# Fifteen one-element reads on GpSimd and a new program order in a fused attention and MLP kernel

## The chip, the cores and the metric

The kernel runs on one core of a Trainium2 chip. The core has five engines, each with its own instruction stream: TensorE (PE) for matrix products, VectorE (DVE) and ScalarE (ACT) for elementwise work, GpSimd (POOL) and SyncE (SP), which here mostly issue DMA transfers. An engine works through its own list in order and waits on semaphores for others. The metric is the time of one execution on the device in microseconds (us), as the median of several runs; one more execution is profiled, and its trace is what the rows below come from.

## The reference

```python
def _attn_ref(q, k, v, n_sink, window):          # q, k, v: (4, 8, 768, 64) f32
    scores = scale * np.matmul(q, k.transpose(0, 1, 3, 2))
    is_sink = pos[None, :] < int(n_sink)         # n_sink = 4
    rel = pos[:, None] - pos[None, :]
    in_window = (rel >= 0) & (rel < int(window)) # window = 128
    scores = np.where(is_sink | in_window, scores, -1e9)
    ...                                          # softmax over the last axis: a
    return np.matmul(a, v)

x = attn_out.transpose(0, 2, 1, 3).reshape(3072, 512)
h = x @ w_in                                     # (512, 2048)
P = a[0] + a[1] * h + a[2] * h**2 + a[3] * h**3
Q = 1.0 + abs(b[0]) * abs(h) + abs(b[1]) * h**2
out = (P / (Q + 1e-6)) @ w_out                   # (2048, 512)
```

Attention with a window of 128 positions and four sink positions, then a layer whose nonlinearity is a quotient of two polynomials, over 4 x 768 = 3,072 tokens.

## The kernel before

The work is cut into 12 steps `s` of 256 tokens, three to a batch. For each step the attention part runs ahead of the matrix part by a step or more:

- `load_q`, `load_k`, `load_v` (L333, L364, L371, and L346, L355, L380 for the first steps) are DMA transfers issued by GpSimd, which cast f32 to bf16 on the way, as do `load_w_in` (four quarters, L412) and `load_w_out` (four, L418). q and k are turned by PE in the first steps (L536) and later by DMA transposes that SyncE issues (`turn_q` L587, `turn_k` L591).
- `scores(s, 0..3)` on PE (L622, L632) puts products of k and q into PSUM and adds the mask by further matmuls (L640); `exps(s, 0..3)` on ACT (L652) takes them to bf16; `attend(s, 0..1)` on PE (L693) multiplies by v; `norm(s, 0..1)` on DVE (L701, L702) divides by the sum and writes the tile `x_n`; `turn_x` (L722, L727 on PE, L740 by DMA from step 5 on) makes `xblk`, the left side of the matrix part.
- `gemm1(m, 0..3)` on PE (L752) is x @ w_in in four quarters of 16 matmuls, each evicted by `copy_in(m, j)` on ACT (L759) into the tile `hb`. The nonlinearity is a chain on DVE and ACT: `sqa`/`sqd` (h squared, ACT L766 or DVE L768), `and` (|h|, L773), `den` (L777), `even` (L782), `odd` (L786), `odd_h` (L790), `num` (L793) on DVE, `ln` (L796) and `exp` (L801) on ACT for the reciprocal, `gate` (L806) on DVE. `gemm2(m, ...)` on PE (L813) is the product with w_out, `copy_out` (L825) its eviction, `store` the transfer to `out`.

`x_n`, `hb`, `sq`, `den`, `g` and `xblk` have two buffers each, `num` has one; a step's tile is written over the tile of two steps before. PSUM is four pools of two banks, `ps_h`, `ps_o`, `ps_m` and `ps_s`; table `BANK` says which pool a product takes.

No scheduler sets the order. Each piece of work is declared with `piece(name, engine, ...)`, which gives it a number; the table `ORDER` is a list of these numbers, and the program is written piece by piece in that order (a negative number -n is n empty matmuls, `spin`). The order of pieces of one engine in `ORDER` is that engine's order of work. Table `ENGINE` says whether a copy goes to DVE or ACT. Semaphores follow from the tiles that a piece reads and writes.

Of the kernel before, what the change touches and what calls it, by code (L numbers as in the profile page):

```python
# [61 lines left out]
def kernel(  # L62
# [42 lines left out]
    V_PE = 3  # L105
    KB = 3
# [7 lines left out]
    ENGINE = {('cast_k0', 0): 'ACT',  # L114
               ('cast_q0', 0): 'DVE',
               ('cast_q0', 1): 'DVE',
               ('place_k0', 0): 'ACT',
               ('place_k0', 1): 'DVE',
               ('place_kc', 2, None): 'ACT',
               ('place_kc', 3, None): 'ACT',  # L120
               ('place_qc', 2, None): 'ACT',
               ('place_qc', 3, 0): 'ACT',
               ('place_vc', 1): 'DVE',
# [3 lines left out]
               ('placed_x', 1, 0): 'DVE',  # L127
               ('placed_x', 2, 0): 'DVE',
               ('placed_x', 4, 0): 'DVE',
               ('placed_x', 4, 1): 'DVE'}  # L130
    BANK = {('attend', 0, 1): 'ps_o',
             ('attend', 2, 0): 'ps_o',
             ('attend', 2, 1): 'ps_h',
             ('attend', 3, 0): 'ps_o',
             ('attend', 3, 1): 'ps_h',
             ('attend', 4, 0): 'ps_o',
# [3 lines left out]
             ('attend', 8, 0): 'ps_o',  # L140
# [5 lines left out]
             ('gemm1', 0, 2): 'ps_o',  # L146
             ('gemm1', 0, 3): 'ps_m',
             ('gemm1', 1, 0): 'ps_m',
             ('gemm1', 1, 1): 'ps_m',
             ('gemm1', 2, 1): 'ps_h',  # L150
# [5 lines left out]
             ('gemm1', 4, 0): 'ps_m',  # L156
# [4 lines left out]
             ('gemm1', 5, 3): 'ps_m',  # L161
             ('gemm1', 6, 0): 'ps_o',
# [6 lines left out]
             ('gemm1', 8, 2): 'ps_o',  # L169
             ('gemm1', 9, 1): 'ps_m',  # L170
# [6 lines left out]
             ('gemm1', 11, 0): 'ps_o',  # L177
# [4 lines left out]
             ('gemm2', 11, 0, 0): 'ps_o',  # L182
             ('scores', 0, 2): 'ps_h',
             ('scores', 1, 1): 'ps_m',
             ('scores', 1, 2): 'ps_o',
             ('scores', 2, 2): 'ps_m',
             ('scores', 2, 3): 'ps_o',
             ('scores', 3, 0): 'ps_h',
             ('scores', 3, 2): 'ps_h',
             ('scores', 4, 1): 'ps_m',  # L190
             ('scores', 4, 3): 'ps_h',
             ('scores', 5, 2): 'ps_o',
             ('scores', 6, 0): 'ps_o',
             ('scores', 6, 2): 'ps_h',
             ('scores', 7, 1): 'ps_o',
             ('scores', 8, 0): 'ps_m',
             ('scores', 8, 1): 'ps_h',
             ('scores', 9, 2): 'ps_h',
# [3 lines left out]
             ('scores', 11, 0): 'ps_m',  # L202
             ('turn_k0', 0): 'ps_h',
             ('turn_k0', 1): 'ps_o',
             ('turn_kc', 2, None): 'ps_h',
             ('turn_kc', 3, None): 'ps_h',
             ('turn_q0', 0): 'ps_m',
             ('turn_qc', 1, None): 'ps_o',
             ('turn_qc', 2, None): 'ps_h',
             ('turn_qc', 3, 0): 'ps_h',  # L210
             ('turn_vc', 1): 'ps_h',
             ('turn_vc', 2): 'ps_h',
             ('turn_vs', 1): 'ps_h',
             ('turn_x', 0, 0): 'ps_o',
             ('turn_x', 0, 1): 'ps_o',
# [3 lines left out]
             ('turn_x', 2, 1): 'ps_h',  # L219
             ('turn_x', 4, 0): 'ps_o',  # L220
# [35 lines left out]
    nil = const_pool.tile([P, 1], FP32, name="nil")  # L256
    sel = const_pool.tile([P, 2, NTS, 64], BF16, name="sel")
# [147 lines left out]
    def place_vc(s, eng):  # L405
        b, g = divmod(s, GPB)
        copy(eng, v_fix[b % 2][:, g * NHF:(g + 1) * NHF, :, 0:D],
             ps_v2.pop(s).rearrange("p j (h d) -> p j h d", d=D))

# [614 lines left out]
    for s in range(NSTEP):  # L1024
# [44 lines left out]
        for G in range(2):  # L1069
# [14 lines left out]
                   ("turned_x", s - 2) if s >= 2 else None], frees=home)  # L1084
        gs = range(2)
        piece(("attended", s), "NONE", 0.0, 0, None, [("attend", s, G) for G in gs])
# [28 lines left out]
    def every(nm, m):  # L1115
        return [(nm, m, p_) for p_ in range(parts(m))] if m >= 0 else []

    for m in range(NSTEP):
        r_ = 4 * m
        old = m - 2  # L1120
        for j in range(4):
            home = bank_of(("gemm1", m, j), ("ps_h", "ps_o")[j % 2])
            piece(("gemm1", m, j), "PE", 1.76, r_ + j,
                  lambda m=m, j=j, home=home: project_in(m, j, home),
                  [("turned_x", m), ("load_w_in", j)], takes=home)
            piece(("copy_in", m, j), "ACT", on_act(GW), r_ + j + 0.25,
                  lambda m=m, j=j: copy_in(m, j),
                  [("gemm1", m, j)] + every("odd_h", old)
                  + ([("turn_vc", s_) for s_ in range(V_PE)] + [("turn_kc", 3, None)]
                     if m == 1 else []),  # L1130
                  frees=home)
# [114 lines left out]
```

## Time and profile before

| | us |
|---|---|
| median of 3 runs | 247.15 (245.81 to 248.28) |
| profiled execution | 248.32 |
| its span, first to last instruction | 246.6 |
| busy in it: PE / DVE / ACT / POOL | 221.3 / 217.1 / 209.7 / 81.5 |

The profiled execution's own time is 1.7 us longer than its span. PE's busy time is that of pipelined matmuls whose ends are modelled, so a busy PE is not PE at its peak. In rows of a timeline the first number is the start, the second the time covered, `xN` the number of equal instructions merged, and the bracket at the end the idle time before the row and what ended it; `issue` means that the profile shows nothing that was waited for.

### The profile page before, as it was taken

What the parts mean: (1) busy time and instruction counts of PE and PEld (TensorE: products, weight loads), DVE (VectorE), ACT (ScalarE), POOL (GpSimd) and SP (SyncE); (2) the same over time, 40 slices, a digit from 0 to 9 for tenths busy, and PEclk for the clock granted to TensorE, in tenths of its full rate; (3) what the DMA queues carried; (4) which work ended last, traced back from release to release, by engine and by line L of the source; (5) the groups of instructions that cost most, each with busy time, mean ns of one, the idle gap of its engine ahead of it and who ended that gap; (6) DMA issues with size and microseconds to landing.
All of it is one profiled execution on the core that took longest, in us unless ns stands there. A gap on an engine that the chain in (4) does not pass through costs nothing.

```text
span 246.6 us, 7309 instructions
## 1 busy us (share of the span) xinstructions
PE 221.3 (90%) x3253; PEld 147.0 (60%) x3253; DVE 217.1 (88%) x252; ACT 209.7 (85%) x173; POOL 81.5 (33%) x111
## 2 busy tenths in 40 slices
PE   1787887995999999699999989999999999999992
PEld 0465665793766667457658647757657668554430
DVE  4977784898779999987898999999999999999991
ACT  2186795998599998978989996999999999999950
POOL 8619567556463896060079600000000000000000
PEclk9999997999799999999999999999999999999999
DMA  7999999999999999999299993053301024000422
GB/s 190 158 184 140 190 181 112 108 101 175 203 156 124 151 186 116 108 173 63 40 96 239 146 98 66 3 66 122 94 3 21 3 44 171 1 3 0 170 85 85
DMA packets 95375, 26.98 MB, mean 109 GB/s; under 512 B 86128, under 2 KB 92272, under 8 KB 95344
## 3 DMA queue, kind: packets, MB, share of 16 engines
q0 software_dynamic: 65024, 12.98, 83.5%
q1 hardware_dynamic: 28792, 12.61, 31.1%
q10 hardware_dynamic: 1528, 0.93, 1.5%
q8 instruction: 25, 0.41, 0.7%
q14 instruction: 6, 0.05, 0.1%
HBM read 27.30 MB, written 6.29 MB: 136 GB/s over the span
## 4 chain that ended last, share of the span: by engine, by line
DVE 44%; PE 34%; issue 8%; ACT 7%; DMA 3%; POOL 1%; SPq 1%; DVEq 0%; POOLq 0%
PE ps_m L752 8%; PE ps_h L813 8%; DVE sq L790 7%; DVE num L793 7%; DVE den L777 5%; PE ps_o L752 5%; DVE g L806 5%; DVE num L782 3%; DMA qT<-q_bf 3%; DVE sq L786 3%; DVE x_n L702 3%; DVE sq L768 3%; ACT hb L759 3%; DVE den L773 2%; PE ps_h L752 2%
## 5 line engine op out<-in xcount | busy, mean ns | idle before, releaser
L752 PEld LDWEIGHTS <-w_in_sb 128*128 128x128 bf16 x768 | 74.5, 99 | 18.3 <-issue 6.2
L813 PE MATMUL ps_h<-w_out_sb,g 128*128 128x512 bf16 x288 | 66.2, 379 | 0.0
L813 PEld LDWEIGHTS <-g 128*128 128x128 bf16 x384 | 36.4, 98 | 42.1 <-DVE g L806 2.6
L796 ACT ACTIVATE lnq<-den,one_eps,qsc 128x4096 f32<-128x4096 bf16 (+1 forms) x18 | 48.3, 2682 | 0.0
L801 ACT ACTIVATE den<-lnq 128x4096 bf16<-128x4096 f32 (+1 forms) x18 | 45.0, 2502 | 0.1
L752 PE MATMUL ps_m<-xblk,w_in_sb 128*128 128x256 bf16 x352 | 43.7, 279 | 0.0
L371 POOL DMA_DIRECT2D v<-in_v_dram x48 | 35.1, 748 | 13.2 <-DVE v L283 7.8
L752 PE MATMUL ps_o<-xblk,w_in_sb 128*128 128x256 bf16 x320 | 38.3, 273 | 0.4 <-ACT hb L759 0.4
L806 DVE TENSOR_TENSOR g<-num,den 128x4096 bf16<-128x4096 bf16 (+1 forms) x18 | 28.3, 1571 | 1.4 <-ACT den L801 1.3
L777 DVE TENSOR_TENSOR den<-den,sq 128x4096 bf16<-128x4096 bf16 (+1 forms) x18 | 28.3, 1573 | 0.8 <-ACT sq L766 0.5
L790 DVE TENSOR_TENSOR sq<-sq,hb 128x4096 bf16<-128x4096 bf16 (+1 forms) x18 | 28.2, 1573 | 0.2
L793 DVE TENSOR_TENSOR num<-num,sq 128x4096 bf16<-128x4096 bf16 (+1 forms) x18 | 28.3, 1572 | 0.1
L759 ACT ACTIVATE hb<-ps_m 128x1024 bf16<-128x1024 f32 x22 | 22.8, 1037 | 6.1 <-PE ps_m L752 6.1
L333 POOL DMA_DIRECT2D q_bf<-in_q_dram x15 | 15.7, 1049 | 32.5 <-DMA qT<-q_bf 27.9
L652 ACT ACTIVATE e<-ps_s 128x768 bf16<-128x768 f32 (+1 forms) x26 | 23.3, 895 | 1.5 <-PE ps_s L640 1.5
L759 ACT ACTIVATE hb<-ps_o 128x1024 bf16<-128x1024 f32 x20 | 20.9, 1047 | 2.0 <-PE ps_o L752 1.9
L766 ACT ACTIVATE sq<-hb 128x1024 bf16<-128x1024 bf16 (+1 forms) x15 | 20.4, 1363 | 0.1
L768 DVE TENSOR_TENSOR sq<-hb 128x2048 bf16<-128x2048 bf16 (+2 forms) x13 | 16.9, 1302 | 2.9 <-ACT hb L759 2.9
L786 DVE TENSOR_SCALAR sq<-sq,acoef 128x4096 bf16<-128x4096 bf16 (+1 forms) x18 | 18.0, 1005 | 0.3
L782 DVE TENSOR_SCALAR num<-sq,acoef 128x4096 bf16<-128x4096 bf16 (+1 forms) x18 | 18.0, 1003 | 0.0
L364 POOL DMA_DIRECT2D k_bf<-in_k_dram x16 | 14.2, 898 | 9.6 <-DMA w_out_sb<-in_moe_w_out_dram 3.5
L773 DVE TENSOR_SCALAR den<-hb 128x2048 uint32<-128x2048 uint32 (+1 forms) x18 | 15.9, 881 | 0.4 <-ACT hb L759 0.4
(131 smaller groups left out, 261.9 us busy)
## 6 DMA issues: line engine op xcount, KB each, us to landing
out_dram<-o_t SPq DMA_DIRECT2D x11, 512.0 KB, 4.8
w_in_sb<-in_moe_w_in_dram POOLq DMA_DIRECT2D x4, 512.0 KB, 9.9
k_bf<-in_k_dram POOLq DMA_DIRECT2D x16, 128.0 KB, 8.0
w_out_sb<-in_moe_w_out_dram POOLq DMA_DIRECT2D x4, 512.0 KB, 14.4
q_bf<-in_q_dram POOLq DMA_DIRECT2D x15, 128.0 KB, 7.8
v<-in_v_dram POOLq DMA_DIRECT2D x24, 64.0 KB, 7.5
stage_v<-in_v_dram POOLq DMA_DIRECT2D x3, 256.0 KB, 8.0
v<-in_v_dram POOLq DMA_DIRECT2D x24, 32.0 KB, 6.6
```

Source lines behind the costliest of these rows:

```text
L371: nc.gpsimd.dma_start(out=v_fix[b % 2][half(r), g * NHF:(g + steps) * NHF, hl, 0:D], in_=v[b, h, g * TS:(g + steps) * TS, :].rearrange("(j ...
L752: nc.tensor.matmul(ps[:, n, :], lhsT=w_in_all[:, c, fc * P:(fc + 1) * P], rhs=xblk[m][:, c, :], start=(c == 0), stop=(c == NDMC - 1))
L759: nc.scalar.activation(out=hb[m][:, j * GW:(j + 1) * GW], in_=ps_h.pop((m, j)).rearrange("p n c -> p (n c)"), func=AF.Copy)
L777: nc.vector.tensor_tensor(out=den[m][:, c], in0=den[m][:, c], in1=sq[m][:, c], op=ALU.add)
L782: nc.vector.tensor_scalar(out=num[m][:, c], in0=sq[m][:, c], scalar1=a2, scalar2=a0, op0=ALU.mult, op1=ALU.add)
L786: nc.vector.tensor_scalar(out=sq[m][:, c], in0=sq[m][:, c], scalar1=a3, scalar2=a1, op0=ALU.mult, op1=ALU.add)
L790: nc.vector.tensor_tensor(out=sq[m][:, c], in0=sq[m][:, c], in1=hb[m][:, c], op=ALU.mult)
L793: nc.vector.tensor_tensor(out=num[m][:, c], in0=num[m][:, c], in1=sq[m][:, c], op=ALU.add)
L796: nc.scalar.activation(out=lnq_fix[:, c], in_=den[m][:, c], func=AF.Ln, scale=qsc, bias=one_eps)
L801: nc.scalar.activation(out=den[m][:, c], in_=lnq_fix[:, c], func=AF.Exp, scale=-1.0)
L806: nc.vector.tensor_tensor(out=g_of[m][:, c], in0=num[m][:, c], in1=den[m][:, c], op=ALU.mult)
L813: nc.tensor.matmul(ps_out[m][:, tt, :], lhsT=g_of[m][:, co:co + P], rhs=w_out_all[:, fc, :], start=(fc == 0), stop=(fc == NFFC - 1))
```

## The change

GpSimd gets 15 new instructions: `hold("x", s)` for steps 0 to 7 copies one element of `x_n` of step s into a small tile `seen`, and `hold("h", m)` for steps 0 to 6 one element of `hb`. Each stands somewhere between GpSimd's load issues. So GpSimd goes no further before `norm(s, 0)` and `norm(s, 1)`, or the four `copy_in(m, j)`, have written their tile; and `norm(s + 2)` and `copy_in(m + 2)`, which write over it, come after the hold. The table `ORDER` is another one throughout (its numbers also shift, since the holds are numbered among the pieces), and tables `ENGINE` and `BANK` change in some rows. There are 3 empty matmuls (`spin`) in place of 19.

```diff
@@ ORDER @@
-    3, 109, 127, 113, 118, -6, 1, 0, 125, 2, 108, 128, 126, 107, 14, 4, 15, 116, 119, 117, 146, 5,
...
+    3, 108, 126, 1, 2, 125, 128, 109, 117, 127, 113, 118, 0, 14, 15, 107, 146, 5, 110, 4, 16, 119,
...
+    HOLD_X = tuple(range(8))
+    HOLD_H = tuple(range(7))
...
-    ENGINE = {('cast_k0', 0): 'ACT',
-               ('cast_q0', 0): 'DVE',
+    ENGINE = {('cast_q0', 0): 'DVE',
                ('cast_q0', 1): 'DVE',
-               ('place_k0', 0): 'ACT',
-               ('place_k0', 1): 'DVE',
+               ('place_k0', 1): 'ACT',
                ('place_kc', 2, None): 'ACT',
                ('place_kc', 3, None): 'ACT',
+               ('place_qc', 0, 0): 'ACT',
+               ('place_qc', 0, 1): 'ACT',
...
-               ('place_vc', 1): 'DVE',
                ('place_vc', 2): 'DVE',
...
+               ('placed_x', 1, 1): 'DVE',
                ('placed_x', 2, 0): 'DVE',
+               ('placed_x', 2, 1): 'DVE',
+               ('placed_x', 3, 1): 'DVE',
...
+    seen = const_pool.tile([1, 2 * NSTEP], BF16, name="seen")
...
+    def hold(kind, s):
+        t_ = x_n[s][0:1, 1, 0:1] if kind == "x" else hb[s][0:1, MW - 1:MW]
+        at = 2 * s + (kind == "x")
+        nc.gpsimd.tensor_copy(out=seen[:, at:at + 1], in_=t_)
...
             piece(("norm", s, G), "DVE", 0.97, 4 * s + at - 5 - 0.1,
                   lambda s=s, G=G: normalize(s, G),
                   [("attend", s, G), ("scale_x",),
-                   ("turned_x", s - 2) if s >= 2 else None], frees=home)
+                   ("turned_x", s - 2) if s >= 2 else None,
+                   ("hold", "x", s - 2) if s - 2 in HOLD_X else None], frees=home)
...
+        if s in HOLD_X:
+            piece(("hold", "x", s), "POOL", 0.2, 4 * s, lambda s=s: hold("x", s),
+                  [("norm", s, 0), ("norm", s, 1)])
...
                   [("gemm1", m, j)] + every("odd_h", old)
+                  + ([("hold", "h", old)] if old in HOLD_H else [])
...
+        if m in HOLD_H:
+            piece(("hold", "h", m), "POOL", 0.2, r_ + 4, lambda m=m: hold("h", m),
+                  [("copy_in", m, j) for j in range(4)])
```

Three places show what the new order moves. The line numbers of the changed kernel are higher by 10 to 15 there.

The first is PE where the first of the long stops fell: 1,214 instructions into its list, in the last mask matmuls of `scores(3, 2)`. Before, `gemm1(0, 3)` follows there; with the change `gemm1(0, 3)` stands ahead of `scores(3, 2)`, and its end falls on that count. ACT's list shows the same exchange in the rows that empty the two products: `copy_in` has `hb<-`, `exps(3, ...)` has `e_1_96` or `e_1_94`. Before:

```order
L766 ACTIVATE sq<-hb 128x1024
L652 ACTIVATE e_1_96<-ps_h 128x2x384
L759 ACTIVATE hb<-ps_m 128x1024
L652 ACTIVATE e_1_94<-ps_s 128x2x384
L652 ACTIVATE e_1_94<-ps_h 128x2x512
L801 ACTIVATE den<-lnq 128x1024
L759 ACTIVATE hb<-ps_m 128x1024
L796 ACTIVATE lnq<-den,one_eps,qsc 128x1024
```

With the change:

```order
L811 ACTIVATE lnq<-den,one_eps,qsc 128x1024
L816 ACTIVATE den<-lnq 128x1024
L774 ACTIVATE hb<-ps_h 128x1024
L667 ACTIVATE e_1_96<-ps_s 128x2x384
L774 ACTIVATE hb<-ps_o 128x1024
L811 ACTIVATE lnq<-den,one_eps,qsc 128x1024
L667 ACTIVATE e_1_94<-ps_s 128x2x384
L667 ACTIVATE e_1_94<-ps_h 128x2x512
```

`copy_in(0, 3)` now comes ahead of `exps(3, 2)`, and `copy_in(1, 0)` ahead of the other two `exps`, as `gemm1(1, 0)` does on PE; they stood behind them.

The second is GpSimd with the loads of v for steps 3 and 4. `v_1` is the v tile of the odd batches; the 64x4x64 loads into it are those of step 3 (one for each head), the 64x8x64 ones of step 4. Before:

```order
L371 DMA v_1_92<-in_v_dram 64x4x64
L333 DMA q_bf_1212<-in_q_dram 128x8x64
L371 DMA v_1_92<-in_v_dram 64x4x64
L371 DMA v_1_92<-in_v_dram 64x8x64 x7
L418 DMA w_out_sb_106<-in_moe_w_out_dram 128x4x512 x4
L364 DMA k_bf_1456<-in_k_dram 128x8x64
```

With the change, from `hold("x", 2)` to the last three quarters of w_out:

```order
L423 COPY seen_117<-x_n_1079 1x1
L381 DMA v_1_92<-in_v_dram 64x8x64
L381 DMA v_1_92<-in_v_dram 64x4x64 x2
L381 DMA v_1_92<-in_v_dram 64x8x64
L381 DMA v_1_92<-in_v_dram 64x4x64 x2
L433 DMA w_out_sb_106<-in_moe_w_out_dram 128x4x512
L423 COPY seen_117<-hb_697 1x1
L381 DMA v_1_92<-in_v_dram 64x8x64 x4
L423 COPY seen_117<-hb_1052 1x1
L423 COPY seen_117<-x_n_1428 1x1
L381 DMA v_1_92<-in_v_dram 64x8x64
L433 DMA w_out_sb_106<-in_moe_w_out_dram 128x4x512 x3
```

Four loads of v step 3 stand behind `hold("x", 2)`, and three quarters of w_out behind `hold("h", 0)`, `hold("h", 1)` and `hold("x", 3)` as well.

The third is ACT around `ln(3)` (`lnq<-den`) and `exp(3)` (`den<-lnq`). The `hb` rows are `copy_in`, the `e_1_94` rows `exps(7, ...)`, the `o_t` row `copy_out(2)`. Before, the first row is `copy_in(4, 3)`, the third `copy_in(4, 2)`:

```order
L759 ACTIVATE hb<-ps_o 128x1024
L796 ACTIVATE lnq<-den,one_eps,qsc 128x4096
L759 ACTIVATE hb<-ps_m 128x1024
L652 ACTIVATE e_0_95<-ps_s 128x2x384
L801 ACTIVATE den<-lnq 128x4096
L652 ACTIVATE e_1_94<-ps_o 128x2x384
L652 ACTIVATE e_1_94<-ps_s 128x2x512
L825 ACTIVATE o_t<-ps_h 128x1024
```

With the change the first two rows are `copy_in(4, 3)` and `copy_in(4, 2)`, the fifth `copy_in(5, 3)`:

```order
L774 ACTIVATE hb<-ps_o 128x1024
L774 ACTIVATE hb<-ps_m 128x1024
L811 ACTIVATE lnq<-den,one_eps,qsc 128x4096
L816 ACTIVATE den<-lnq 128x4096
L774 ACTIVATE hb<-ps_o 128x1024
L840 ACTIVATE o_t<-ps_h 128x1024
L667 ACTIVATE e_1_94<-ps_m 128x2x512
L667 ACTIVATE e_1_94<-ps_s 128x2x384
```

`copy_in(4, 2)`, `exp(3)` and a quarter of step 5 stand ahead of the first `exps(7, ...)`; on PE `gemm1(4, 2)`, `gemm1(5, 3)` and the first half of `gemm2(2, 1)` stand likewise ahead of `scores(7, 1)`, which stood ahead of `gemm1(4, 2)`.

## Rows read from the trace of the kernel before

**Rows 1.** The page's first lines: the span, then busy us of each engine.

```profile
span 246.6 us, 7309 instructions
PE 221.3 (90%) x3253; PEld 147.0 (60%) x3253; DVE 217.1 (88%) x252; ACT 209.7 (85%) x173; POOL 81.5 (33%) x111
```

**Rows 2.** Windows: stretch, length, busy PE, PEld, DVE, ACT, POOL, clock, DMA, GB/s.

```profile
24.00:70.00 46.00, 39.28 (x816) 30.22 (x814) 34.99 (x59) 36.32 (x42) 27.09 (x34) 0.93 1.95 153
70.00:150.00 80.00, 76.78 (x1146) 49.98 (x1144) 75.37 (x64) 75.02 (x54) 39.33 (x48) 1.00 1.87 128
150.00:240.00 90.00, 89.26 (x959) 56.10 (x957) 88.56 (x79) 86.36 (x63) 0.00 (x0) 1.00 0.20 57
```

**Rows 3.** The timeline of DVE: four rows of norm from 20 to 70 us.

```profile
20.91 0.75 DVE L702 SCALAR_TENSOR_TENSOR x_n<-ps_m,ratio,rec 128x512 bf16<-128x512 f32 x1
...
42.98 0.21 DVE L701 RECIPROCAL rec<-ps_o 128x8 f32<-128x8 f32 x1 [3.05 <-PE ps_o L693]
...
48.13 0.75 DVE L702 SCALAR_TENSOR_TENSOR x_n<-ps_h,ratio,rec 128x512 bf16<-128x512 f32 x1
...
69.45 0.21 DVE L701 RECIPROCAL rec<-ps_o 128x8 f32<-128x8 f32 x1 [3.34 <-PE ps_o L693]
```

**Rows 4.** The timeline of PE: two gemm1 pieces and the four stops.

```profile
28.94 1.92 PE L752 MATMUL ps_o<-xblk,w_in_sb 128*128 128x256 bf16 x16
...
38.52 0.35 PE L640 MATMUL ps_h<-nege,ident 64*64 64x256 bf16 x2 [1.54 <-issue]
38.80 3.49 PE L752 MATMUL ps_m<-xblk,w_in_sb 128*128 128x256 bf16 x16
...
46.36 0.27 PE L632 MATMUL ps_s<-qT,kT 64*64 64x192 bf16 x2 [0.41 <-issue]
...
61.63 2.53 PE L752 MATMUL ps_h<-xblk,w_in_sb 128*128 128x256 bf16 x15 [2.51 <-issue]
...
147.34 0.25 PE L693 MATMUL ps_o<-v,e 64*64 64x65 bf16 x6 [1.03 <-issue]
```

**Rows 5.** Windows up to the first two stops, and behind the first.

```profile
0.00:38.50 38.50, 25.37 (x607) 18.86 (x607) 29.35 (x74) 23.95 (x30) 24.43 (x43) 1.00 1.45 173
0.00:46.30 46.30, 32.80 (x735) 23.92 (x735) 33.99 (x83) 28.73 (x36) 28.61 (x48) 0.96 1.59 160
...
39.90:43.00 3.10, 3.10 (x80) 2.19 (x78) 0.05 (x2) 0.67 (x1) 2.62 (x4) 0.65 2.12 98
```

**Rows 6.** The instruction queue: whole run, then 43.0 to 43.3, 148.4 to 148.7 us.

```profile
q8 instruction: 25, 0.41, 0.7%
...
q8 instruction: 1, 0.02, 36.5%
...
q8 instruction: 1, 0.02, 22.6%
```

**Rows 7.** The timeline of DVE: place_vc(1).

```profile
23.92 1.22 DVE L554 CAST v<-ps_h 128x1024 bf16<-128x1024 f32 x1
```

**Rows 8.** The page's v issues on GpSimd, DMA landings; timeline: attend(3,1) on PE.

```profile
L371 POOL DMA_DIRECT2D v<-in_v_dram x48 | 35.1, 748 | 13.2 <-DVE v L283 7.8
...
w_in_sb<-in_moe_w_in_dram POOLq DMA_DIRECT2D x4, 512.0 KB, 9.9
...
v<-in_v_dram POOLq DMA_DIRECT2D x24, 32.0 KB, 6.6
...
56.69 0.25 PE L693 MATMUL ps_h<-v_sink,e 64*64 64x130 bf16 x4
```

**Rows 9.** Timelines of PE, ACT and DVE: the waits from 104 to 113 us.

```profile
104.99 0.36 PE L632 MATMUL ps_o<-qT,kT 64*64 64x192 bf16 x8 [2.19 <-DMA qT<-q_bf]
...
107.34 1.02 ACT L759 ACTIVATE hb<-ps_m 128x1024 bf16<-128x1024 f32 x1 [1.33 <-PE ps_m L752]
...
108.40 1.76 DVE L768 TENSOR_TENSOR sq<-hb 128x3072 bf16<-128x3072 bf16 x1 [0.73 <-ACT hb L759]
...
112.61 2.29 DVE L806 TENSOR_TENSOR g<-num,den 128x4096 bf16<-128x4096 bf16 x1 [1.31 <-ACT den L801]
```

More of the change, by code (lines that the diff above doesn't have):

```diff
@@ L127 @@
                ('placed_x', 1, 0): 'DVE',
+               ('placed_x', 1, 1): 'DVE',
                ('placed_x', 2, 0): 'DVE',
+               ('placed_x', 2, 1): 'DVE',
+               ('placed_x', 3, 1): 'DVE',
                ('placed_x', 4, 0): 'DVE',
                ('placed_x', 4, 1): 'DVE'}
-    BANK = {('attend', 0, 1): 'ps_o',
-             ('attend', 2, 0): 'ps_o',
-             ('attend', 2, 1): 'ps_h',
+    BANK = {('attend', 0, 0): 'ps_h',
+             ('attend', 0, 1): 'ps_o',
+             ('attend', 1, 1): 'ps_h',
+             ('attend', 2, 1): 'ps_o',
              ('attend', 3, 0): 'ps_o',
              ('attend', 3, 1): 'ps_h',
-             ('attend', 4, 0): 'ps_o',
+             ('attend', 4, 0): 'ps_h',
              ('attend', 5, 1): 'ps_o',
@@ L139 @@
              ('attend', 7, 0): 'ps_o',
-             ('attend', 8, 0): 'ps_o',
+             ('attend', 8, 1): 'ps_o',
              ('attend', 9, 0): 'ps_o',
@@ L145 @@
              ('attend', 11, 0): 'ps_o',
-             ('gemm1', 0, 2): 'ps_o',
-             ('gemm1', 0, 3): 'ps_m',
-             ('gemm1', 1, 0): 'ps_m',
+             ('gemm1', 0, 0): 'ps_o',
+             ('gemm1', 0, 2): 'ps_m',
+             ('gemm1', 0, 3): 'ps_h',
+             ('gemm1', 1, 0): 'ps_o',
              ('gemm1', 1, 1): 'ps_m',
+             ('gemm1', 1, 2): 'ps_m',
+             ('gemm1', 2, 0): 'ps_o',
              ('gemm1', 2, 1): 'ps_h',
@@ L155 @@
              ('gemm1', 3, 3): 'ps_m',
-             ('gemm1', 4, 0): 'ps_m',
+             ('gemm1', 4, 0): 'ps_o',
              ('gemm1', 4, 1): 'ps_m',
@@ L160 @@
              ('gemm1', 5, 2): 'ps_m',
-             ('gemm1', 5, 3): 'ps_m',
-             ('gemm1', 6, 0): 'ps_o',
              ('gemm1', 6, 2): 'ps_o',
@@ L169 @@
              ('gemm1', 8, 2): 'ps_o',
+             ('gemm1', 8, 3): 'ps_m',
              ('gemm1', 9, 1): 'ps_m',
@@ L176 @@
              ('gemm1', 10, 3): 'ps_m',
-             ('gemm1', 11, 0): 'ps_o',
+             ('gemm1', 11, 0): 'ps_m',
              ('gemm1', 11, 2): 'ps_m',
@@ L181 @@
              ('gemm2', 9, 0, 0): 'ps_o',
-             ('gemm2', 11, 0, 0): 'ps_o',
-             ('scores', 0, 2): 'ps_h',
-             ('scores', 1, 1): 'ps_m',
+             ('scores', 0, 0): 'ps_h',
+             ('scores', 0, 1): 'ps_m',
+             ('scores', 0, 3): 'ps_m',
+             ('scores', 1, 1): 'ps_h',
              ('scores', 1, 2): 'ps_o',
+             ('scores', 1, 3): 'ps_h',
              ('scores', 2, 2): 'ps_m',
-             ('scores', 2, 3): 'ps_o',
+             ('scores', 2, 3): 'ps_m',
              ('scores', 3, 0): 'ps_h',
[L189 to L193, printed above, removed]
+             ('scores', 4, 1): 'ps_h',
+             ('scores', 5, 1): 'ps_o',
+             ('scores', 5, 2): 'ps_m',
+             ('scores', 6, 0): 'ps_h',
              ('scores', 6, 2): 'ps_h',
-             ('scores', 7, 1): 'ps_o',
+             ('scores', 7, 0): 'ps_m',
              ('scores', 8, 0): 'ps_m',
              ('scores', 8, 1): 'ps_h',
+             ('scores', 8, 2): 'ps_o',
              ('scores', 9, 2): 'ps_h',
@@ L201 @@
              ('scores', 10, 3): 'ps_o',
-             ('scores', 11, 0): 'ps_m',
+             ('scores', 11, 1): 'ps_m',
              ('turn_k0', 0): 'ps_h',
-             ('turn_k0', 1): 'ps_o',
+             ('turn_kc', 1, None): 'ps_o',
              ('turn_kc', 2, None): 'ps_h',
-             ('turn_kc', 3, None): 'ps_h',
-             ('turn_q0', 0): 'ps_m',
+             ('turn_kc', 3, None): 'ps_o',
              ('turn_qc', 1, None): 'ps_o',
-             ('turn_qc', 2, None): 'ps_h',
+             ('turn_qc', 2, None): 'ps_o',
              ('turn_qc', 3, 0): 'ps_h',
-             ('turn_vc', 1): 'ps_h',
+             ('turn_vc', 1): 'ps_o',
              ('turn_vc', 2): 'ps_h',
-             ('turn_vs', 1): 'ps_h',
-             ('turn_x', 0, 0): 'ps_o',
-             ('turn_x', 0, 1): 'ps_o',
+             ('turn_vs', 0): 'ps_h',
+             ('turn_vs', 1): 'ps_o',
+             ('turn_x', 0, 0): 'ps_h',
              ('turn_x', 1, 0): 'ps_o',
@@ L219 @@
              ('turn_x', 2, 1): 'ps_h',
+             ('turn_x', 3, 1): 'ps_h',
              ('turn_x', 4, 0): 'ps_o',
```

76 rows, old and new, of the table ORDER are left out of this document.

## The prediction

> **What bounds the kernel now.** I read the busy times first, then the same by stretch, then PE's timeline where it stops, then the waits of VectorE (DVE) and ScalarE (ACT). The span is 246.6 us and DVE is busy for 217.1 of it [rows 1]. By stretch, DVE is idle 11.0 of the 46 us from 24 to 70, 4.6 of the 80 us to 150 and 1.4 of the 90 us to 240 [rows 2]. So from 70 us on the kernel is a chain of DVE work, and what can still be won lies ahead of 70 and in a few gaps behind it.
>
> Ahead of 70, DVE waits for TensorE (PE). Its two longest waits there, 3.05 us at 42.98 and 3.34 us at 69.45, are both for an attend matmul [rows 3], so PE sets the pace. PE itself stops inside a piece of work, for "issue": 1.54 us in the mask matmuls of scores(3,2), 0.41 us in scores(3,3), 2.51 us after one matmul of gemm1(2,1), 1.03 us in attend(8,0) [rows 4]. Nothing in the data flow ends there. The place does: between the first two stops lie 256 PE instructions (607 and 607, then 735 and 735) [rows 5], and 25 packets of the instruction queue, 0.41 MB, serve some 6,500 PE instructions, 16 KB for about 260 [rows 6]. I read this as: PE's code comes in blocks of 256, and PE stops at a block's end until the next is there. The next fetch starts late while loads run: at 43.0 to 43.3, over 4.5 us behind the stop that ended at 38.52; at 148.4 to 148.7, at most 1.4 us behind the one that ended at 147.34, with the loads over [rows 4, 6]. With loads a block so takes 46.36 - 38.52 = 7.8 us, and the next two together 61.63 - 46.36 = 15.3 us [rows 4], whatever little work they hold. I call the stops at 38.5, 46.4 and 61.6 ends 4, 5 and 7, since ends lie every 256 instructions of PE's list.
>
> **The change part by part.** PE's order is the same in large parts, only eight instructions (spins) shorter, so each block holds nearly the same pieces; what moves is which lie just ahead of an end.
>
> *Front and copies, 0.* Copies of the first q, k and v tiles change places between DVE and ACT; the largest, place_vc(1), takes 1.22 us off DVE [rows 7]. It lies in the stretch where DVE has 11.0 us to spare, so I cost it at nothing: what would be gained is waited for at the next attend. GpSimd loads w_in's third quarter behind hold("x",0), that is behind norm(0,0), which ended at 21.7; at the median of 9.9 us from issue to landing it is there at 31.6, and gemm1(0,2) started at 28.94: 2.7 us late at the worst [rows 3, 4, 8]. The two loads that now stand ahead of it stood right behind it before and were under way by 28.94 as well, so I take 0 and keep 2.7 for the range; a little gain from the earlier casts, 0.3 us as a guess, is the other end.
>
> *Block ends from 38 to 70 us, 0 (-3.5 to +3.0).* gemm1(0,3) now runs ahead of end 4 instead of behind it, in the time in which PE stood still. That wins 1.9 us of work for PE [rows 4], but nothing at end 5: if the fetch sets it, it stays near 46.4, with less to do before it. Between the ends are then scores(3,2), gemm1(1,0), attend(2,0), two scores and a fifth of attend(2,1), some 4 us of work for 7.8 us. So the stop grows from 0.4 to over 3 us. After the stop of 1.54 us at end 4 the granted clock was 0.65 from 39.9 to 43.0, a mix of 2.4 and 1.2 GHz [rows 5], and the gemm1 there took 3.49 us instead of 1.92 [rows 4]. I expect the same 1.57 us behind end 5, in a block that is full (attend(2,1), four gemm1), so that end 6 comes 1.6 to 2 us later than before. The block behind it is again short, with a stop of 2.51 us in it to give [rows 4]; and GpSimd now has fewer loads out, since three of the four w_out quarters went behind hold("x",3). I take both together as giving the 2 us back, so that norm(4,0) starts where it did, at 69.45. The lower end: of the 6.4 us that DVE waits for the two attends [rows 3], a fetch as quick as that at 148 gives back about half. The upper: 1.6 for the clock and 1.4 for v tiles (third rival).
>
> *Behind 70 us, -2.0 (-2.0 to 0).* PE waited 2.19 us at 104.99 for a q transpose before scores(7,1). gemm1(4,2) stood behind that, ACT waited 1.33 us for it at 107.34, and DVE lost 0.73 us at 108.40 and 1.31 us at 112.61 [rows 9]. Now gemm1(4,2), gemm1(5,3) and a piece of gemm2 stand ahead of scores(7,1), some 4 us of work, so the transpose lands under them: 0.73 + 1.31 = 2.0. It is nothing if load_q(15), which now stands behind two v loads that wait for attend(5,1), comes late.
>
> *The holds, +0.5 (0 to +1.0).* Fifteen reads of one element on GpSimd: no such row exists; between nothing and a load's issue of 0.75 us [rows 8] each they are at most 11 us on an engine busy 81.5 of 246.6 [rows 1]. What counts is the waits they add. GpSimd stands until a norm or a copy_in is done, with loads behind it; norm(s+2) and copy_in(m+2) then wait for the hold, and have two steps for that, of some 20 us each (12 in 240). The tightest chain is on SyncE: turn_x(8) now stands behind turn_k(11,1), whose load is ten issues behind hold("h",6); 10 x 0.75 + 6.6 [rows 8] is 14 us, inside the two steps between copy_in(6) and gemm1(8). Half a microsecond for all of them together.
>
> The sum is 0 + 0 - 2.0 + 0.5 = -1.5 us. The profiled execution took 248.32 us; 246.8 with the change. The median of the runs, 247.15, lies 1.17 lower, so I predict 245.6.
>
> **The rivals.**
> *Paced loads bring the code sooner.* With GpSimd held at norms, fewer loads are out when PE crosses an end, and the 4.5 us shrink towards 1.4. For it: that difference [rows 6]. Against: around 38 to 43 us the loads behind hold("x",1) run just then, and the transposes on SyncE still follow them. It would give the lower end, -3.5, with -1.5 from the rest: 242.1. The Trainium skill (DMA: Bandwidth & Descriptors, Queues, rings and completion order) says that a DMA engine takes turns between queue rows, a packet each; by that rule a fetch in its own row would not stand behind a backlog and pacing would give nothing. The trace disagrees by 4.5 against 1.4 us, so I keep the rival.
>
> *Slower: v tiles behind a hold.* Four of the eight loads of v step 3 now stand behind hold("x",2), that is behind norm(2,1), done at 48.9 [rows 3]. The last is the sixth in line: 48.9 + 5 x 0.75 + 6.6 = 59.3 [rows 8], and attend(3,1) started at 56.69 [rows 8]: up to 2.6 us late, 1.4 once attend(3,1) itself is pushed back by the slow clock. With the 1.6 us of the clock, and no later gain since load_q(15) follows attend(5,1), it is +3.0: 250.2. It decides from the point where the last v load lands later than PE arrives and the stop at end 7 is not long enough to hide it. For it: both numbers; against: GpSimd starts again with an empty line of loads after such a hold, and the 6.6 was taken behind longer lines.
>
> *Nothing that can be measured.* The holds end before GpSimd gets to them, and the stops move from one end to another: 0, or 247.2. For it: PE's list hardly changes. The Trainium skill (Runtime: NRT & Kernel Launch, Instruction fetch mechanics) says that crossing a 16 KiB boundary is mostly hidden, by which rule the blocks could cost nothing here either way. The four stops [rows 4] speak against the rule, not against the result.
>
> **How the numbers follow.** Forecast 0.45, paced loads 0.28, slower 0.15, nothing 0.12. About 1%, 2.5 us, is what a measurement of this kernel can tell from no change. Faster by more than that is under 244.7: all of the second case and a sixth of the first, 0.35. Slower is over 249.6: 0.15. The rest, 0.50, is within 1%. The range takes in 242.1 with a microsecond below it and reaches to just short of the slower case, which with the tails is the 2 in 10 left out: 241.0 to 249.8. The forecast's own range is 244 to 248.
>
> **What would show it.** Right: in the changed profile a gemm1 ends just ahead of a short stop near 38.5; a stop of 3 us or more near 46 inside attend(2,1), with a granted clock under 1 behind it; DVE's norm(4,0) within a microsecond of 69.5; no wait of PE for qT near 105, and no idle DVE from 107 to 113. Wrong: the stop near 46 is short, or ends before 44 (second case); attend(3,1) waits for a v load (third); PE or ACT waits for the GpSimd holds anywhere behind 70; or DVE's idle time from 70 to 240 grows over 6.0 us, which no term here has.

## The result and the profile after

The changed kernel took 240.31 us (median of six, 239.22 to 242.89), the kernel before 248.26 beside it (six, 245.81 to 248.94). The ratio is 0.970, 95% interval 0.9635 to 0.9764. I had predicted 245.6, range 241.0 to 249.8: below the range, and nearest to the rival of the paced loads. (Ratios leave out executions disturbed by a lower clock, so they differ from the ratio of the medians, by up to 1.4% below.)

The page's first lines, then the windows of [rows 2], of the kernel after:

```profile
span 238.9 us, 7325 instructions
PE 217.6 (91%) x3249; PEld 146.7 (61%) x3249; DVE 215.2 (90%) x253; ACT 210.0 (88%) x172; POOL 92.7 (39%) x126
```

```profile
24.00:70.00 46.00, 41.92 (x914) 33.66 (x906) 39.92 (x68) 42.17 (x46) 29.11 (x39) 1.00 1.91 148
70.00:150.00 80.00, 79.99 (x1266) 52.94 (x1265) 77.03 (x67) 77.22 (x57) 49.09 (x58) 1.00 1.83 128
150.00:240.00 90.00, 83.33 (x792) 50.67 (x789) 82.46 (x75) 79.83 (x57) 0.00 (x0) 0.99 0.23 66
```

The span is 7.7 us shorter. From 24 to 70 us DVE is idle 6.1 us in place of 11.0, from 70 to 150 us 3.0 in place of 4.6, and in this execution no clock under 1.00 is left ahead of 150. DVE's timeline, the row of norm(4,0), against 69.45 in [rows 3]:

```profile
64.78 0.21 DVE L716 RECIPROCAL rec<-ps_h 128x8 f32<-128x8 f32 x1 [0.34 <-PE ps_h L708]
```

So 4.7 us were won ahead of it and 3.0 behind it. PE's timeline where [rows 4] has its stops:

```profile
37.95 1.91 PE L767 MATMUL ps_h<-xblk,w_in_sb 128*128 128x256 bf16 x16
...
40.18 1.92 PE L767 MATMUL ps_o<-xblk,w_in_sb 128*128 128x256 bf16 x16
...
43.51 0.51 PE L708 MATMUL ps_o<-v,e 64*64 64x65 bf16 x24
...
58.43 0.36 PE L647 MATMUL ps_m<-qT,kT 64*64 64x192 bf16 x8 [1.84 <-DMA kT<-k_bf]
```

```profile
0.00:39.30 39.30, 25.91 (x606) 20.29 (x607) 26.88 (x72) 24.61 (x31) 20.13 (x38) 1.00 1.26 161
0.00:43.60 43.60, 30.21 (x734) 23.67 (x735) 31.02 (x79) 28.87 (x36) 23.71 (x42) 1.00 1.45 159
```

The windows count as many instructions as [rows 5] (606 and 734 matmuls for 607 and 735, and the same 607 and 735 weight loads): ends 4 and 5 now lie at 39.3 and 43.6, 4.3 us apart and not 7.8, and neither has a stop. The gemm1 behind end 4 (now gemm1(1,0)) takes 1.92 us, where the one there before took 3.49. The instruction queue, in 40.5 to 40.8 and in 52.4 to 52.6 us, against [rows 6]:

```profile
q8 instruction: 1, 0.02, 27.9%
...
q8 instruction: 1, 0.02, 37.1%
```

The packet behind end 4 comes 1.2 us behind it (before: over 4.5), the one behind end 6 (52.07) 0.4 us. The longest wait of PE that is left behind 24 us is the 1.84 us above, for a k transpose. That the stops are waits for these packets shows in all 16 traces together: up to 150 us there are 29 stops of 0.3 us or more at such ends, and after each of them PE began again 1.2 to 1.7 us behind the end of the last packet. GpSimd's waits, summed by line:

```profile
POOL seen L423 <- DVE x_n L717: 22.1, 4, 9.6
POOL seen L423 <- DMA qT<-q_bf: 9.5, 1, 9.5
POOL seen L423 <- ACT hb L774: 9.5, 1, 9.5
```

GpSimd stands 41.1 us at the reads (it waits at six of them for long); the profile puts down no wait of PE, ACT or DVE to them.

### The profile page after: what moved, and what is told of

The parts are those of the page before. It is cut to its first block, busy times and chain, and to the rows that moved or that the text cites. A ratio compares the mean times of both kernels' runs of the same rounds, so it can differ in the third digit from the quotient of the medians.

```text
span 238.9 us, 7325 instructions
## 1 busy us (share of the span) xinstructions
PE 217.6 (91%) x3249; PEld 146.7 (61%) x3249; DVE 215.2 (90%) x253; ACT 210.0 (88%) x172; POOL 92.7 (39%) x126
## 4 chain that ended last, share of the span: by engine, by line
PE 52%; ACT 21%; DVE 10%; DMA 6%; POOL 4%; issue 4%; SPq 2%; POOLq 0%; DVEq 0%; ACTq 0%
PE ps_h L828 18%; PE ps_o L767 9%; PE ps_m L767 8%; ACT hb L774 5%; ACT lnq L811 5%; PE ps_m L828 4%; DMA kT<-k_bf 3%; ACT e L667 3%; ACT den L816 3%; ACT sq L781 2%; PE ps_h L767 2%; DMA v<-in_v_dram 2%; DVE g L821 2%; PE ps_m L708 2%; SPq L602 1%
## 5 line engine op out<-in xcount | busy, mean ns | idle before, releaser
L767 PEld LDWEIGHTS <-w_in_sb 128*128 128x128 bf16 x768 | 73.7, 98 | 14.7 <-issue 3.5
L767 PE MATMUL ps_m<-xblk,w_in_sb 128*128 128x256 bf16 x352 | 42.1, 273 | 0.5 <-ACT hb L774 0.3
L767 PE MATMUL ps_o<-xblk,w_in_sb 128*128 128x256 bf16 x336 | 40.2, 273 | 0.0
L774 ACT ACTIVATE hb<-ps_o 128x1024 bf16<-128x1024 f32 x21 | 21.8, 1038 | 3.3 <-PE ps_o L767 3.2
L667 ACT ACTIVATE e<-ps_s 128x768 bf16<-128x768 f32 (+1 forms) x25 | 22.1, 884 | 0.0
L708 PEld LDWEIGHTS <-e 64*64 64x64 bf16 x1216 | 13.3, 107 | 6.0 <-issue 4.7
```

What stands on the lines that cost most here:

```text
L667: nc.scalar.activation(out=data, in_=ps[:, :, c0:512], func=AF.Exp, scale=inv_sqrt_d)
L767: nc.tensor.matmul(ps[:, n, :], lhsT=w_in_all[:, c, fc * P:(fc + 1) * P], rhs=xblk[m][:, c, :], start=(c == 0), stop=(c == NDMC - 1))
L774: nc.scalar.activation(out=hb[m][:, j * GW:(j + 1) * GW], in_=ps_h.pop((m, j)).rearrange("p n c -> p (n c)"), func=AF.Copy)
```

## The experiments

After the result I had two theories: the reads pace the loads, or the new order alone makes the gain. "None", "early" and "late" below are the changed kernel without any read, with the six ahead of 60 us, with the nine behind. x1 stands for `hold("x", 1)`, h6 for `hold("h", 6)`. "Loads out" are loads that GpSimd has issued and that have not landed. The kernel before ran again beside every group of runs, with medians of 248.72 to 249.23, and the ratios are to it.

**No reads.**
```diff
     def hold(kind, s):
+        if True:
+            return
```


> The changed kernel with its order, engines and banks, but with none of the fifteen reads on GpSimd. Paced loads (my theory now): GpSimd again runs ahead with its loads, the packets of PE's code come 3.5 to 5 us behind ends 4 to 6 as in the kernel before, norm(4,0) starts near 69, and the time is 244 to 247 us. Order alone (rival): the gain comes from where the pieces lie against the ends of the blocks; the packets come as soon as in the changed kernel (0.4 to 2.7 us at ends 3 to 6), norm(4,0) starts near 65, and the time is 239 to 241.5.

Measured: 250.68 us (four; ratio 1.0146 to the kernel before, interval 1.0062 to 1.0229). The new order alone is slower than the old one, by about 1.5%; on it the reads are worth 10 us by the medians, where I had expected 4 to 7. norm(4,0) is at 68.08, but most is lost later. PE's timeline of this run, with scores(9,2) the second row, and the chain of waits ahead of it:

```profile
128.12 0.36 PE L710 MATMUL ps_m<-v,e 64*64 64x65 bf16 x24
133.07 0.54 PE L649 MATMUL ps_h<-qT,kT 64*64 64x192 bf16 x8 [4.59 <-DMA qT<-q_bf]
...
134.77 3.60 PE L769 MATMUL ps_o<-xblk,w_in_sb 128*128 128x256 bf16 x16
```

```profile
124.25 8.69 DMA qT<-q_bf
```

Its DMA view, first 110 to 123 us, then 123 to 140 (queue, packets, MB, share; issues with their landing):

```profile
q0 software_dynamic: 262, 0.03, 4.0%
...
q0 software_dynamic: 7420, 0.92, 151.2%
q1 hardware_dynamic: 3806, 0.91, 86.3%
...
v<-in_v_dram POOLq DMA_DIRECT2D x7, 64.0 KB, 8.0
...
qT<-q_bf SPq DMA_TRANSPOSE x4, 8.1
```

GpSimd's last loads (load_k(11,0) and what follows) start at 120.7, just as SyncE issues its transposes. Both then take 8 us (medians), PE stands 4.59 us, and the gemm1 behind takes 3.60 us for 1.9: the granted clock is 0.57 from 133 to 140 us, so mostly the lower level of 1.2 GHz. q0 holds the loads; the transposes, and a store, are in q1.

**The old order with six reads.**
```diff
+    HOLDS = {("load_w_in", 0): ("x", 0), ("load_v", 4, 7): ("x", 1), ("load_v", 3, 4): ("x", 2),
+             ("load_v", 4, 5): ("h", 0), ("load_v", 4, 6): ("h", 1), ("load_k", 7, 0): ("x", 3)}
     names = list(work)
     for n in ORDER:
+        if n >= 0 and names[n] in HOLDS:
+            hold(*HOLDS[names[n]])
```


> The kernel before with its own order, and six reads of GpSimd put between its load issues at places like those of the change: x0 ahead of load_w_in(0), x1 ahead of load_v(4,7), x2 ahead of load_v(3,4), h0 and h1 ahead of load_v(4,5) and load_v(4,6), x3 ahead of load_k(7,0). Paced loads: the packets come 1 to 3 us behind ends 4 to 6 in place of 4.4 to 5.0, norm(4,0) starts at 65 to 67, and the time is 243 to 246 us. Order alone: 247.5 to 249, unchanged. Slower is possible, 249 to 251, if the v tiles behind x2 come late for attend(3,1).

Measured: 244.97 us (nine; before 248.72; ratio 0.9934, interval 0.9882 to 0.9986, so clear of no change only just), norm(4,0) at 66.77, both as expected. The packets came 3.92, 0.81 and 0.31 us behind ends 4 to 6: later than I expected at one, and sooner at two. At end 4, right behind x1, the loads issued ahead of it were still out, and PE stopped 1.81 us.

**Early reads alone, late reads alone.**
```diff
+        if (kind, s) not in (("x", 0), ("x", 1), ("h", 0), ("x", 2), ("h", 1), ("x", 3)):
+            return
```


> The changed kernel with only its first six reads (x0, x1, x2, h0, h1, x3), all ahead of 60 us. Paced loads: the gain stands whole ahead of 70 us, norm(4,0) near 65, time 239.5 to 241.5, as the changed kernel. If the later reads help as well (code or transposes that come sooner behind 70): 241.5 to 243. Order alone: 239 to 241.5 here too, so this run speaks only together with the one that has no reads.

> The changed kernel without its first six reads, with the nine later ones (h2, x4 to x7, h3 to h6). Paced loads: as without any, norm(4,0) near 69 and 244 to 247 us. Order alone: 239 to 241.5. If the late reads are what matters: under 241.5 with norm(4,0) near 69.

Measured: early 248.17 us (ten; ratio 0.9985, interval 0.9927 to 1.0043), late 243.95 (four; 0.989, 0.9769 to 1.0011). The first expectation missed, and the second was met at the edge of its range (244) but with norm(4,0) at 67.23: the late reads carry more than the early ones, 6.7 us of the 10 against 2.5 by the medians. With early reads alone the wait ahead of scores(9,2) is there (5.35 us), with late ones it is 0.34. With late ones alone the stops ahead of 70 are there. PE's timeline of that run, at ends 5 and 7:

```profile
45.58 0.35 PE L710 MATMUL ps_o<-v,e 64*64 64x65 bf16 x19 [1.15 <-issue]
...
60.44 0.24 PE L639 MATMUL ps_s<-qT,k_sink 128*32 128x128 bf16 x3 [2.60 <-issue]
```

The packets came 4.4 us behind ends 5 and 6 there, where the changed kernel has 2.7 and 0.4.

**One read: h6. All but h6 and x7.**
```diff
+        if (kind, s) != ("h", 6):
+            return
```
The second run has `in (("h", 6), ("x", 7))` there.

> The changed kernel with one read of its fifteen, h6, behind which the last v loads stand (load_v(9,4) and all after it). Theory now: the large gain is made at one place, where these loads would run at the same time as the transposes that scores(9,2) waits for; without any read turn_q(18) took 8.69 us from 124.25 and PE stood 4.59 us at 133. So with h6 alone PE does not stand there, the block of PE's code that starts near 122 takes under 7 us in place of 9.9, and the time is 243 to 245.5, as with the nine late reads (243.95). Rival: the nine late reads help a little each: 247 to 249.5.

> The changed kernel without h6 and x7, with the other thirteen reads. Theory: the last v loads run beside the transposes again, PE stands 3 to 5 us ahead of scores(9,2), the clock is at half for some us behind it, and the time is 245.5 to 248, nearly all of the late loss. Rival, x6 and h5 ahead of them already hold these loads back far enough: 240 to 242.

Measured: h6 alone 245.05 us (four, 241.74 to 248.95; 0.9777, 0.9705 to 0.9849), as expected: 5.6 of the 10 us by one read, a rough size with four executions that far apart. PE has no wait ahead of scores(9,2). SyncE's list is the same as without reads, and the transposes that it issues from 121 to 124 us land in 3.5 to 4.1 us in place of 6.3 to 7.2. The DMA view of 121 to 124 us, first with h6, then without any read:

```profile
kT<-k_bf SPq DMA_TRANSPOSE x2, 4.1
qT<-q_bf SPq DMA_TRANSPOSE x1, 3.5
```

```profile
kT<-k_bf SPq DMA_TRANSPOSE x2, 7.2
qT<-q_bf SPq DMA_TRANSPOSE x1, 6.3
```

GpSimd's last v loads start at 135.2 us there, behind h6, and not at 121.6. All but h6 and x7: 244.91 (four, 242.79 to 247.25; 0.9778, 0.9721 to 0.9835), 0.6 us under the range that I expected; PE waits 1.79 us there, not 4.59. That h5 and x6, which stand ahead of h6, hold part of these loads back is likely, but was not tried by itself.

**Seven reads.** The same filter, letting x1, x2, h0, h1, x3, h6 and x7 through.

> The changed kernel with seven of its fifteen reads: x1, x2, h0, h1, x3 (the code of ends 5 and 6) and h6, x7 (the transposes near 125). Theory: these carry the whole gain, 239.5 to 241.5. Rival: x0 or the reads between 70 and 110 us carry a part, 242 to 245.

Measured: 240.73 us (six; 0.9697, 0.9656 to 0.9739), as with all fifteen. As expected.

**No reads, transposes earlier.**
```diff
+    order = list(ORDER)
+    first = [("turn_k", 9, 1), ("turn_q", 20), ("turn_k", 9, 0), ("turn_q", 18)]
+    for nm in first:
+        order.remove(names.index(nm))
+    at = order.index(names.index(("turn_x", 6, 1)))
+    order[at:at] = [names.index(nm) for nm in first]
+    for n in order:
```


> The changed kernel without any read, with four transposes on SyncE (turn_k(9,1), turn_q(20), turn_k(9,0), turn_q(18)) put ahead of turn_x(6,1), where SyncE stood idle from 101 to 116 us. Theory (the loss near 133 is a wait for transposes that share the DMA engines with loads): PE no longer stands ahead of scores(9,2), and the time is 243 to 246, without any read. Rival (the late reads do something else, such as the code's packets coming sooner): 249 to 251, as without reads.

Measured: 244.26 us (four; 0.9852, 0.9783 to 0.992). The wait for a transpose is gone with no read at all, and 6.4 us with it. Issued from 100 to 107 us, the first two of the moved transposes took 10.6 and 9.1 us, longer than the 6.3 to 8.7 us without the move, but PE did not have to wait for them. So what costs time is a transpose that lands too late. Together with the rows of h6 alone: what h6 does near 125 us is to keep v loads from running beside these transposes.

**Without x1; with x1, h6, x7.** The same filter.

> The changed kernel with six reads: x2, h0, h1, x3, h6, x7, so without x1, behind which the loads of 36 to 42 us stand. If x1 keeps the line of loads short for end 5: the stop at end 5 is back at 1 us or more (it was 1.34 us without any early read, 0.12 in the changed kernel), end 6 still has its code at once (x2, h0, h1), and the time is 241 to 243, 1 to 2 us over the kernel with seven reads (240.73). Rival, x1 does nothing that x2 doesn't do: 240 to 241.

> The changed kernel with three reads: x1, h6, x7, so without x2, h0, h1 and x3, which hold back the w_out quarters and the v loads of 46 to 60 us. If the depth of the line of loads sets how late PE's code comes: no stop at end 5, but the packet behind end 6 comes 3.5 to 4.5 us late again (0.37 in the changed kernel), PE stops 2 to 3 us at end 7, and the time is 241.5 to 244. Rival, x1 alone makes the early gain: 240 to 241.

Measured: without x1 241.27 us (four, 239.67 to 242.88; 0.98, 0.9707 to 0.9893). The stop at end 5 did not come back: GpSimd had run through these loads, and all but one had landed before end 4. In the profiled execution, the longest of the four, end 4 itself came at 42.5 us, 3.2 us later than with seven reads, with a clock of 0.72 from 38 to 44 us. The time lies in the first range, though not for its reason, and 0.5 us from that of seven reads: whether x1 by itself is needed these runs don't tell. Without x2, h0, h1 and x3: 244.12 (four; 0.989, 0.9813 to 0.9968), 3.4 us more than with seven; the packet behind end 6 is 2.85 us late and the stop at end 7 0.7 us, both less than expected. The larger loss I had not expected. The chain, then PE's timeline:

```profile
51.26 10.77 DMA kT<-k_bf
```

```profile
62.08 0.54 PE L649 MATMUL ps_m<-qT,kT 64*64 64x192 bf16 x8 [4.03 <-DMA kT<-k_bf]
...
62.76 3.59 PE L769 MATMUL ps_h<-xblk,w_in_sb 128*128 128x256 bf16 x16
```

PE waits 4.03 us for a k transpose of 10.77 us beside the w_out and v loads, and the gemm1 behind takes 3.59 us (clock 0.50 from 62 to 67 us), where the changed kernel's chain has

```profile
50.40 7.99 DMA kT<-k_bf
```

**Can the remaining wait go? Loads of v step 4 later, and the change once more.**
```diff
+    move(("load_w_out", 0), ("load_v", 4, 4))
+    move(("load_v", 4, 6), ("hold", "h", 1))
+    move(("load_v", 4, 7), ("hold", "h", 1))
+    move(("load_v", 4, 2), ("hold", "x", 3))
+    move(("load_v", 4, 0), ("hold", "x", 3))
```
Each load is put right behind the second name.

> The changed kernel with all its reads; behind x2 only the four v tiles that attend(3,1) needs, two v tiles of step 4 behind h0, two behind h1, three and then the w_out quarters behind x3. Of the changed kernel's waits this goes for the 7.99 us that the k transpose of 50.40 took beside those loads, and PE's 1.84 us at 58.43 for it. If loads in flight slow the transposes: the transpose takes 3 to 5 us, the wait is gone, 238.5 to 240. If not: 240 to 241. Slower, 241 to 243, if a v tile of step 4 or the first w_out quarter comes late for attend(4,0) or gemm2(0,0,0).

> The changed kernel itself once more, on the chip of the runs beside it, as what the version with the v tiles of step 4 later is to be compared with: 239.5 to 241.

Measured: 244.17 us (twelve; 0.9946, 0.9896 to 0.9995), beside 243.62 for the change again (seven; 0.9752, 0.9673 to 0.9832), three of its executions at 239.7 to 240.5 and four at 243.6 to 244.7. Both missed: none of the twelve is under 243.4. The transpose, now issued at 51.28 us, was no quicker than about 7 us; PE's wait at 58 shrinks to 0.69 us in the main because PE gets there 1.2 us later. And PE now waits for w_out as well (the brackets):

```profile
58.47 0.36 PE L647 MATMUL ps_m<-qT,kT 64*64 64x192 bf16 x8 [0.69 <-DMA kT<-k_bf]
...
68.10 1.04 PE L828 MATMUL ps_h<-w_out_sb,g 128*128 128x512 bf16 x3 [0.70 <-DMA w_out_sb<-in_moe_w_out_dram]
...
70.63 1.02 PE L828 MATMUL ps_h<-w_out_sb,g 128*128 128x512 bf16 x4 [1.49 <-DMA w_out_sb<-in_moe_w_out_dram]
```

**Transposes moved, with all reads and with seven.** The move of the run without reads, and turn_k(4,0) ahead of turn_q(9).

> The changed kernel with all its reads; on SyncE turn_k(4,0) is put ahead of turn_q(9), so that turn_k(5,0) is issued 1.25 us sooner, and turn_k(9,1), turn_q(20), turn_k(9,0), turn_q(18) ahead of turn_x(6,1). In the run of the changed kernel that was looked at last (241.9 us of span) PE stood 1.5 us for a q transpose near 125, and blocks 7 and 14 took 10.07 and 6.92 us in place of 8.38 and 5.29. If transposes that come late are what remains: PE's waits for transposes fall under 0.7 us each and the time is 238.5 to 240.5 in nearly all runs. Rival, the spread comes from the clock or the code at the front: 240 to 244 as before.

> The same moved transposes with only seven reads (x1, x2, h0, h1, x3, h6, x7). If the reads do nothing but keep loads apart from transposes and code: 238.5 to 240.5, as with all reads. Rival, with the transposes moved the eight other reads count: 1 us or more above the kernel with all of them.

Measured: 246.14 us with all reads (twelve; 0.9863, 0.9803 to 0.9923), 241.41 with seven (six; 0.9764, 0.9697 to 0.9831). Both missed. With all reads turn_q(18) stands ahead of turn_x(6,1) but its load behind the reads h3 and x5: it lands at 116.6 us, SyncE waits 5.8 us for it, and the x transposes come late. PE's timeline:

```profile
59.37 0.36 PE L647 MATMUL ps_m<-qT,kT 64*64 64x192 bf16 x8 [3.28 <-DMA kT<-k_bf]
...
126.78 1.91 PE L767 MATMUL ps_o<-xblk,w_in_sb 128*128 128x256 bf16 x16 [1.43 <-DMA xblk<-x_n]
```

turn_k(5,0) was issued at 50.44 as before (the second q transpose ahead of it stood until its load landed, at 49.1 us), and PE waited longer for it.

What makes the changed kernel's executions differ by 4 us is in part in its two traces, of 238.9 and 241.9 us. At 56 us they are level. In the second PE then waits 1.94 us in place of 1.84 for the k transpose, and the gemm1 behind runs at a lower clock (0.73 from 60 to 66 us, 1.00 in the first):

```profile
58.94 2.73 PE L767 MATMUL ps_h<-xblk,w_in_sb 128*128 128x256 bf16 x16
```

That makes norm(4,0) 1.7 us late, and a wait of 1.45 us for a q transpose at 128 us does most of the rest. Whether the other executions differ in the same way no trace tells. No version tried beats the change clearly.

The two places, from DVE's timeline of each profiled execution (us; "between" is from norm(4,0) to the first norm of step 8):

| kernel | median | norm(4,0) | between |
|---|---|---|---|
| before | 248.3 to 249.2 | 69.45 | 77.4 |
| old order, six reads | 244.97 | 66.77 | 76.4 |
| new order, none | 250.68 | 68.08 | 79.8 |
| early | 248.17 | 68.63 | 80.6 |
| late | 243.95 | 67.23 | 72.8 |
| h6 | 245.05 | 68.84 | 72.7 |
| none, transposes earlier | 244.26 | 66.66 | 73.5 |
| seven | 240.73 | 64.15 | 72.9 |
| all (the change) | 240.31 | 64.78 | 73.1 |
| the change again | 243.62 | 66.48 | 74.1 |
| all but h6, x7 | 244.91 | 65.69 | 74.4 |
| six, without x1 | 241.27 | 66.04 | 73.8 |
| x1, h6, x7 | 244.12 | 71.01 | 72.7 |
| v of step 4 later | 244.17 | 64.82 | 78.6 |
| all, transposes moved | 246.14 | 67.30 | 74.1 |
| seven, transposes moved | 241.41 | 63.94 | 74.3 |

The row "early" comes from an execution of 252.25 us, its longest: PE stood 1.41 us at 21.4 and 1.93 us at 60.7 in it. On the new order the last column tells the late gain apart: against no reads or early ones alone it is 5 to 8 us with h6 or with the transposes out of the way, and with the v loads of step 4 later most of it is lost again to other waits. Not tried is the old order with late reads too, so how much of the gain needs the new order stays open.

For PE's code I took ends 0 to 16 of all 16 traces (272): the time from PE's first instruction behind an end to the next 16 KB packet, by how many loads were out (the landing from their bytes in the software queue).

| loads out | ends | median us | middle half |
|---|---|---|---|
| 0 or 1 | 46 | 0.95 | 0.45 to 1.2 |
| 2 or 3 | 70 | 1.7 | 0.3 to 2.7 |
| 4 or 5 | 85 | 2.6 | 1.8 to 3.7 |
| 6 or more | 71 | 3.7 | 3.1 to 4.1 |

The middle halves overlap, and the rows mix places in the program. At one place alone, end 5, the order is nearly the same over the 16 traces: 0.7 and 0.8 us with one load out, 2.1 to 3.0 with three, 3.9 to 4.4 with six. At end 4 it is not (0.1 to 3.9 us with three out).

## Why the prediction was wrong

*Front and copies, 0.* Within its bounds: end 4 came 0.8 us later. The w_in load behind x0 was no danger: with only two loads still out, which landed 0.6 and 2.1 us later, it landed in 5.4 us, not 9.9.

*Block ends from 38 to 70 us, 0 (-3.5 to +3.0).* This is the step that failed: -4.7. I saw that the fetch comes 4.5 us late under loads and 1.4 without, and still kept 4.5 for end 5, because loads would run behind x1 too. By the table above it is in the main the number out that counts, and behind a read fewer are: 3 or 4 at ends 4 to 6 of the change, 5 to 7 before. So the stop of over 3 us at end 5, its half clock and the later end 6 did not come; nor did the third rival (attend(3,1) had no wait).

*Behind 70 us, -2.0.* The size was near (-3.0 for all that lies behind norm(4,0)), the reason incomplete. The wait at 104.99 went, but DVE still waits 0.86 and 0.98 us near 100 and 112:

```profile
99.10 1.76 DVE L783 TENSOR_TENSOR sq<-hb 128x3072 bf16<-128x3072 bf16 x1 [0.86 <-ACT hb L774]
...
111.95 0.21 DVE L716 RECIPROCAL rec<-ps_m 128x8 f32<-128x8 f32 x1 [0.98 <-PE ps_m L708]
```

And the new order brings a wait of 4.6 us ahead of scores(9,2) that no term had; in the change the reads prevent it. So that the size came out near is partly luck.

*The holds, +0.5.* Wrong in sign, and the second step that failed: as an addition to the new order they are worth -10. I priced the waits that they add, of which the trace of the change shows none outside GpSimd, and left their use to a rival.

*Paced loads, 0.28.* The right rival, its gain priced too small (242.1): it had the code but not the transposes. How the early gain divides between code and transposes the runs don't tell apart: with x2, h0, h1 and x3 away, both come late. The Trainium skill (DMA: Bandwidth & Descriptors, Queues, rings and completion order) lets a DMA engine take turns between queue rows; by that a transpose or a fetch in a row of its own would share the engine with the loads, but not stand behind their backlog. The 8.69 and 10.77 us above, for 2.5 in a quiet stretch, speak against leaning on that here; what in the DMA engines or on the way to them makes the delay, no run tells.

## What to carry to other kernels

Where loads are issued far ahead of their use, look at what else goes through the DMA engines meanwhile: here transposes and TensorE's code came late beside a deep line of loads, and a wait of the issuing engine, for which nothing else had to wait, brought them forward. Price such a wait by what it keeps apart, not only by what stands behind it. And an order found together with such waits should be judged with them: alone it was slower here, by 1.5%.

## What I had not expected of the hardware

A transpose whose issue takes 1.2 us needed 2.5 us to land in a quiet stretch [the kernel before, 110 to 123 us] and 6 to 11 us beside a deep line of loads. Ten loads in 17 us, seven of them v tiles of 64 KB, were enough for the 8.69 us [the kernel without reads, 123 to 140 us]: nearly all packets there are under 512 bytes, and the times of the 0.92 MB in the loads' queue add up to 151% of the stretch on all 16 engines.
